# A sparse-attention and gated-convolution kernel: the first V on the software queue, mask rows by SBUF transfers, closing blocks in halves

## The chip, the core and the metric

The kernel runs on one core of a Trainium2 chip. The core has a matrix engine (TensorE, here PE; its weight loads, PEld, overlap its matmuls), VectorE (DVE), ScalarE (ACT), GpSimd (POOL) and SyncE (SP). Each engine runs its own instructions in the order in which the program put them down, and waits for other engines and for transfers by semaphores. Transfers (DMAs) are issued from SP and ACT, which have one hardware queue each, and from POOL, whose software queue also converts types on the way. All of them run on the same 16 DMA engines.

The metric is device time in microseconds. The kernel before takes 208.67 us, the median of three runs (208.65 to 208.9).

## What is computed

Block-sparse attention for 4 batch elements of 8 heads, 768 tokens and 64 channels, and behind it a gated convolution layer. Cut to what matters:

```python
scores = scale * np.matmul(q, k.transpose(0, 1, 3, 2))
mask = np.abs(blk_i - blk_j) <= window                    # blocks of 32 tokens
mask = mask | (blk_i == 0) | (blk_j == 0) | (blk_i == n_blocks - 1) | (blk_j == n_blocks - 1)
for qb in range(n_blocks):
    for kb in sampled_blocks[qb]:
        mask[qb * block:(qb + 1) * block, kb * block:(kb + 1) * block] = True
scores = np.where(mask, scores, -1000000000.0)
attn = softmax(scores)
x = np.matmul(attn, v)                                    # then heads side by side: 768 x 512 a batch element
h = np.maximum(x @ w_in, 0.0)                             # 512 -> 1024
conv_out = sum(conv_w[k] * shifted(h, k) for k in range(3))
out = h * sigmoid(conv_out) @ w_out                       # 1024 -> 512
```

`sampled_blocks` gives three more key blocks for each of the 24 query blocks. All heads share one mask.

## The kernel before

**Scores and mask.** Heads are taken in pairs, 16 pairs P = 0 to 15, four to a batch element. For each pair there is a slot, a tile t of 88 rows: rows 0 to 63 hold q and k transposed (24 chunks of 128 tokens: 12 of q, 12 of k), rows 64 to 87 hold 24 mask rows. With them one matmul (line 761) gives the scores and adds a large negative number where a query block may not see a key block: the q side carries the table of forbidden block pairs, the k side says which block a key is of. The mask rows are the same for every pair. There are five slots; pairs 0 to 4 are the first to use them.

**Units.** A unit is eight score blocks of 128 x 128: two score steps on PE into one of two PSUM tiles st, one exponential on ACT (line 773) into one of six tiles pt, and two steps of products with V on PE (line 798) into av. There are 144 units. They are ordered in segments: half of the queries (g = 0 or 1) of one batch element at a time. In the first segment a pair takes 4.5 units: unit 2 is the first that needs head 1 of pair 0, the second half of unit 4 is the first of pair 1, unit 9 the first of pair 2, the second half of unit 13 the first of pair 3.

**The layer behind.** Normalised rows (line 709) are transposed to xT; 18 units after its attention a segment goes through f1 (line 895), relu, the convolution on DVE (lines 953, 961) or, for the last segment, on PE (line 972), tanh on ACT, the gate gT (line 1008), and f2 (line 830) by `out_block`: for each block of 128 tokens eight matmuls of 512 columns, an eviction (ev) to a tile o2s and a store of 256 KB. Only the very last block is made in two halves of 256 columns.

**The order.** The steps are entered in a graph by `op` and `dma`, and numbered in that sequence. The string ORDER lists all 1,787 steps by two-character numbers; where a step may run on several engines a letter names one, and for a step that allocates a buffer a character gives its index. `put_down` follows that string. So the order on every engine, SP and POOL with their transfers among them, is written out by hand, and the costs and due times given in the source only served to find it.

**The start.** Pair 0 is loaded in 32 bits by the hardware queues: k in two halves (SP and ACT), q in two halves (ACT and SP), with the table of sampled blocks (`ld_sb`, SP, into sbi) ahead of the second half of q, then both heads of V (`ld_v0`, SP, into a tile of m) and the convolution weights (`ld_cw`). Casts on ACT and DVE (`cast_q`, `cast_k`) and PE transposes follow; `k_cp` and `q_cp` copy the transposes from PSUM into the slot. POOL makes iota and ident and then issues the loads of pairs 1, 2 and so on through the software queue. DVE builds the table of pairs: a1, a3 (from iota), a4 (first use of sbi), a5 in two halves into mtok (line 299). `nblk` (from ident) gives the k side. Mask rows are written into slot 0 by copies: `m_k` (k side, head 0), `m_q0` (q side, g = 0), `m_q1` (g = 1), `m_h1` (head 1: one copy of the q side, one of the k side), `m_r1` (g = 1 of head 1). Then `m_slot` copies all 24 rows from slot 0 to each of slots 1 to 4 on DVE. `m_back` stores a reordered copy for later pairs by two transfers from SP. `v_cp` brings V of pair 0 from 32 bits into its tile vt, on ACT between exponentials 1 and 2.

## Time and profile before

| | us |
|---|---|
| median of the runs | 208.67 |
| lowest and highest run | 208.65, 208.9 |
| span of the profiled execution, first to last instruction | 206.8 |

The page has no time of the profiled execution other than its span; 1.9 us of the median lie outside it. The granted TensorE clock is 0.997 of full speed over the span. The costliest groups of instructions, with busy time, mean duration of one in ns, and idle time of the engine ahead of them with what ended it:

```profile
L773 ACT ACTIVATE pt<-st 128x1024 bf16<-128x1024 f32 x144 | 140.6, 1048 | 2.4 <-PE st L761 1.3
L761 PE MATMUL st<-t 88*128 88x256 bf16 (+2 forms) x600 | 90.0, 267 | 1.6 <-ACT t L327 0.8
...
L798 PE MATMUL av<-vt,pt 128*128 128x65 bf16 x1152 | 58.4, 193 | 0.0
L895 PE MATMUL mix<-xT,winb 128*128 128x384 bf16 (+2 forms) x288 | 54.3, 308 | 0.3 <-ACT hE L915 0.2
```

Matmuls overlap, so the busy times of PE's groups add up to more than PE's busy time. `t<-mix` means that tile t is written from tile mix, buffer numbers left out.

### The profile page before, as it was taken

The page shows a single profiled execution, that of the slowest core. Times are in us where ns is not written, and L with a number is a line of the kernel's source. Part 1 is how long each engine was busy: PE and PEld are TensorE (multiplying, and loading weights), DVE is VectorE, ACT ScalarE, POOL GpSimd, SP SyncE. Part 2 cuts the span into 40 slices and gives each one's busy share as a digit, 9 for nine tenths or more (in the row PEclk, how much of TensorE's full clock was granted, in tenths as well). Part 3 has the DMA queues.
Part 4 walks back from the last instruction along what each step waited for, and adds up shares of the span by engine and source line. Part 5 has one row for each costly group of instructions (what it writes and reads, how often), then busy time and mean ns, then how long its engine had stood idle before and what let it go on. Part 6 is the DMA issues. An engine that isn't in the chain of part 4 may idle for free.

```text
span 206.8 us, 6250 instructions
## 1 busy us (share of the span) xinstructions
PE 199.3 (96%) x2418; PEld 142.7 (69%) x2418; DVE 186.4 (90%) x576; ACT 190.6 (92%) x252; POOL 61.9 (30%) x113
## 2 busy tenths in 40 slices
PE   7799999999999999999999999999999999999992
PEld 5587878887567766766676767676667667786750
DVE  7999989999999998999789989999999938999970
ACT  6999999999999999999989998999999979997751
POOL 8696735302843233316054153800000000000000
PEclk9999999999999999999999999999999999999998
DMA  6999999998699976999969659999235131010414
GB/s 156 196 196 185 181 165 132 187 113 77 78 127 142 179 102 93 147 139 193 194 96 107 138 77 170 151 144 130 67 115 87 22 120 51 3 51 5 152 53 153
DMA packets 49305, 25.20 MB, mean 122 GB/s; under 512 B 35100, under 2 KB 46332, under 8 KB 49276
## 3 DMA queue, kind: packets, MB, share of 16 engines
q0 software_dynamic: 19728, 11.05, 44.9%
q1 hardware_dynamic: 29260, 13.46, 33.9%
q8 instruction: 19, 0.31, 0.6%
q10 hardware_dynamic: 288, 0.30, 0.4%
q14 instruction: 10, 0.08, 0.1%
HBM read 23.09 MB, written 6.29 MB: 142 GB/s over the span
## 4 chain that ended last, share of the span: by engine, by line
PE 71%; DVE 14%; ACT 11%; issue 2%; ACTq 0%
PE st L761 22%; PE mix L830 18%; PE mix L895 16%; PE av L798 12%; ACT pt L773 8%; DVE t L331 3%; DVE m L953 3%; DVE m L961 2%; DVE gT L1008 1%; ACT t L327 1%; DVE xtok L709 1%; PE st L830 1%; DVE hE L917 1%; PE mix L728 1%; DVE m L1003 1%
## 5 line engine op out<-in xcount | busy, mean ns | idle before, releaser
L773 ACT ACTIVATE pt<-st 128x1024 bf16<-128x1024 f32 x144 | 140.6, 1048 | 2.4 <-PE st L761 1.3
L761 PE MATMUL st<-t 88*128 88x256 bf16 (+2 forms) x600 | 90.0, 267 | 1.6 <-ACT t L327 0.8
L761 PEld LDWEIGHTS <-t 88*128 88x128 bf16 x600 | 48.5, 97 | 21.4 <-issue 1.6
L798 PEld LDWEIGHTS <-pt 128*128 128x128 bf16 x1152 | 52.2, 97 | 11.5 <-ACT pt L773 1.0
L798 PE MATMUL av<-vt,pt 128*128 128x65 bf16 x1152 | 58.4, 193 | 0.0
L895 PE MATMUL mix<-xT,winb 128*128 128x384 bf16 (+2 forms) x288 | 54.3, 308 | 0.3 <-ACT hE L915 0.2
L953 DVE TENSOR_SCALAR m<-hE,cw 128x382 bf16<-128x382 bf16 (+2 forms) x192 | 48.8, 316 | 0.4
L830 PE MATMUL mix<-woutb,gT 128*128 128x512 bf16 x184 | 48.7, 379 | 0.2 <-DVE gT L1008 0.2
L961 DVE TENSOR_TENSOR m<-m 128x764 bf16<-128x764 bf16 (+2 forms) x64 | 33.8, 534 | 0.6
L895 PEld LDWEIGHTS <-winb 128*128 128x128 bf16 x288 | 24.4, 97 | 9.4 <-issue 0.8
L1000 ACT ACTIVATE m<-m 128x764 bf16<-128x764 bf16 (+2 forms) x32 | 26.8, 840 | 1.1 <-DVE m L961 1.0
L407 POOL COPY pace<-pt 1x1 bf16<-1x1 bf16 x24 | 9.6, 402 | 53.3 <-ACT pt L773 53.3
L830 PEld LDWEIGHTS <-gT 128*128 128x128 bf16 x200 | 17.3, 97 | 11.7 <-DVE gT L1008 1.1
L915 ACT ACTIVATE hE<-mix 128x384 bf16<-128x384 f32 (+2 forms) x36 | 17.7, 507 | 1.7 <-PE mix L895 1.6
L917 DVE TENSOR_SCALAR hE<-mix 128x384 bf16<-128x384 f32 x28 | 15.5, 557 | 4.1 <-PE mix L895 3.7
L1008 DVE TENSOR_TENSOR gT<-m,hE 128x764 bf16<-128x764 bf16 (+3 forms) x36 | 18.2, 511 | 0.6
L709 DVE TENSOR_TENSOR xtok<-av,rcp 128x384 bf16<-128x384 f32 (+2 forms) x36 | 18.1, 508 | 0.5
L239 POOL DMA_DIRECT2D nat<-in_q_dram x23 | 17.0, 738 | 2.1 <-issue 1.4
L331 DVE COPY t<-mix 64x384 bf16<-64x384 bf16 (+1 forms) x33 | 13.4, 413 | 0.7 <-PE mix L522 0.2
L327 ACT COPY o2s<-mix 128x512 f32<-128x512 f32 x17 | 9.9, 598 | 2.9 <-PE mix L830 2.7
L1003 DVE TENSOR_SCALAR m<-m 128x764 bf16<-128x764 bf16 (+3 forms) x36 | 12.1, 335 | 0.5 <-ACT m L1000 0.4
L239 POOL DMA_DIRECT2D vn<-in_v_dram x15 | 11.3, 756 | 1.9 <-DVE vt L331 1.4
(75 smaller groups left out, 118.4 us busy)
## 6 DMA issues: line engine op xcount, KB each, us to landing
out_dram<-o2s SPq DMA_DIRECT2D x23, 256.0 KB, 2.9
nat<-in_k_dram POOLq DMA_DIRECT2D x15, 192.0 KB, 4.2
vn<-in_v_dram POOLq DMA_DIRECT2D x15, 192.0 KB, 5.7
nat<-in_q_dram POOLq DMA_DIRECT2D x6, 192.0 KB, 4.9
winb<-in_moe_w_in_dram POOLq DMA_DIRECT2D x2, 512.0 KB, 7.3
woutb<-in_moe_w_out_dram POOLq DMA_DIRECT2D x4, 256.0 KB, 6.7
nat<-in_q_dram POOLq DMA_DIRECT2D x9, 96.0 KB, 5.2
nq<-in_q_dram POOLq DMA_DIRECT2D x6, 96.0 KB, 5.1
```

Of the source, the lines that this page charges most:

```text
L239: return op(name, {eng: occ}, lambda e: on(e).dma_start(out=dst(), in_=src), prio, deps, dma=(kind, service), **kw)
L331: nc.vector.tensor_copy(out=dst, in_=src)
L709: nm = op("norm", {"DVE": t_dps(128 * C)}, lambda e: nc.vector.tensor_tensor(out=xtok_t[xk.index][:, 0:C].rearrange("p c h d -> p h c d"), ...
L761: nc.tensor.matmul(out=st[:, 128 * x:128 * (x + n_)], lhsT=t[0:88, 12 + 6 * hh + kc, :], rhs=t[0:88, idx:idx + (n_ - 1) * (2 if P < NPE el ...
L773: nc.scalar.activation(out=pt_t[ptb.index][:, c0:c1], in_=st_t[stb.index][:, c0:c1], func=AF.Exp, bias=0.0, scale=0.125)
L798: nc.tensor.matmul(out=o[:, off:off + 65], lhsT=pt_t[ptb.index][:, 128 * x:128 * x + 128], rhs=V_t[vslot_b[P].index][:, hh, kc, 0:65], sta ...
L830: nc.tensor.matmul(out=acc(), lhsT=gT_t[gb.index][:, ffc, 128 * t:128 * t + 128], rhs=woutb[:, ffc, c0:c1], start=(ffc == 0), stop=(ffc == ...
L895: nc.tensor.matmul(out=mix_t[hb.index][:, w1 * y:w1 * y + w1], lhsT=winb[:, fc, 128 * ffc:128 * ffc + 128], rhs=xT_t[xt_buf[n].index][:, f ...
L953: nc.vector.tensor_scalar(out=m_t[cb.index][:, x, y, 0:w], in0=hE_t[heb.index][:, f0 + y, t0 + x:t0 + x + w], scalar1=cw[:, x, f0 + y:f0 + ...
L961: nc.vector.tensor_tensor(out=m[:, a_, :, 0:w], in0=m[:, a_, :, 0:w], in1=m[:, b_, :, 0:w], op=ALU.add)
L1000: th = [op("tanh", {"ACT": t_act(2 * w) + 0.04}, lambda e, cb=cb, w=w: nc.scalar.activation(out=m_t[cb.index][:, 0, :, 0:w], in_=m_t[cb.in ...
L1008: nc.vector.tensor_tensor(out=gT_t[gtb.index][:, f0:f0 + 2, t0:t1], in0=m_t[cb.index][:, 0, :, 0:w], in1=hE_t[heb.index][:, f0:f0 + 2, 1 + ...
```

## The change

- `ld_sb` moves from SP to POOL, ahead of iota; the second half of q follows k at once on SP.
- `ld_v0`, its 32-bit tile and its cast are gone. V of pair 0 is loaded by the software queue like that of the other pairs, behind q of pair 1, and `v_cp` copies it from 16 bits on either engine.
- The k side of head 1 (`m_hk`), the g = 1 rows of head 1 (`m_r1`) and the mask rows of slots 1 to 4 (`m_sk`, two `m_sq` and two `m_sr` for slot 1, `m_sp` for slots 2, 3 and 4) are written by transfers within SBUF, issued from SP, in place of copies on DVE.
- The scores of g = 1 wait for their own rows only.
- For the last batch element the blocks t = 3 and t = 4 are made in halves of 256 columns, as t = 5 is.
- ORDER is written anew as a whole, with 1,803 steps.

In the new string SP has, from the start: k, q, `m_hk`, `ld_cw`, `m_sq`, `m_sq`, `m_sk`, `m_r1`, `m_back`, `m_sp` (slot 2), `m_sr`, `m_sr`, `m_sp` (slot 4), `m_sp` (slot 3), then the transposing transfers. POOL has `ld_sb`, iota, ident, k and q of pair 1, V of pair 1, V of pair 0, k of pair 2 and on. ACT has `m_k`, three casts, `q_cp`, `m_q0`, two `k_cp`, and exponentials from there on. DVE has a1, nblk, a3, a4, `m_k`, the first a5, `k_cp`, `m_q0`, `k_cp`, `m_h1`, `cast_q`, the second a5, `q_cp`, `m_q1`, four copies for pair 1, ident24, `v_cp` of pair 0. PE has the scores of units 0 to 5 ahead of the first product with V. On PE the last steps are f2 of t = 3 and t = 4, second halves.

```diff
 ORDER = """
-0J0K1c1f00021010P0Q1Q01R0R0S0T0310V0/A0U14V1b0I0L0M0N0V0W0X1xA11zA1AA0405060708090a0b0c0d0e0f0g0h0i0j0k0l0m0n0o
...
+000L0O010P0J0K1U01g1f1V02103042401S10I0M05060708090a0b0c0d0e0f0Q0S1j0R1e1h2611O0272012i22k20+A1AA31CA1DA0g0h0i0j0k
...
-    vf = m_t[0].rearrange("p x y s -> p (x y s)")[:, 0:1536].bitcast(FP32)
...
-    ld_sb = op("ld_sb", {"SP": 0.46}, lambda e: nc.sync.dma_start(
-        out=sbi[64:MR], in_=sampled_blocks.bitcast(I32).rearrange("b r -> (b r)").unsqueeze(0).broadcast_to([NB, 6 * NB])),
-        -21, after=[k0], lat=1.8)
-    q1 = first_q(1, "SP", -20, [ld_sb])
+    ld_sb = dma("ld_sb", "POOL", lambda: sbi[64:MR], sampled_blocks.bitcast(I32).rearrange("b r -> (b r)").unsqueeze(
+        0).broadcast_to([NB, 6 * NB]), -21, kind="sw")
+    q1 = first_q(1, "SP", -20, [k0])
     ld_q0, ld_k0 = [q0, q1], [k0, k1]
-    ld_v0 = dma("ld_v0", "SP", lambda: vf.rearrange("p (h c) -> p h c", h=2),
-                v[0, 0:2].rearrange("h (p c) d -> p h (c d)", p=128), -18, service=1.6, after=[q1])
...
+    def rows_dma(name, prio, deps, dst, src):
+        return dma(name, "SP", dst, src, prio, deps, service=0.25)
+
+    def two_heads(x):
+        return x.unsqueeze(1).broadcast_to([NB, 2] + list(x.shape)[1:])
+
     m_h1 = [op("m_h1", {"DVE": 0.25, "ACT": 0.37}, lambda e: dcopy(e, T_t[0][64:88, 6:11:2], T_t[0][64:88, 0:5:2]), T(0), m_q),
-            op("m_h1", {"DVE": 0.45, "ACT": 0.69}, lambda e: dcopy(e, T_t[0][64:88, 18:24], T_t[0][64:88, 12:18]), T(0), m_k)]
-    m_r.append(op("m_r1", {"DVE": 0.25, "ACT": 0.37}, lambda e: dcopy(
-        e, T_t[0][64:88, 7:12:2], T_t[0][64:88, 1:6:2]), -5, m_r[0:1]))
+            rows_dma("m_hk", T(-2), m_k, lambda: T_t[0][64:88, 18:24].rearrange("j c s -> j (c s)"),
+                     T_t[0][64:88, 12:18].rearrange("j c s -> j (c s)"))]
+    m_r.append(rows_dma("m_r1", T(2), m_r[0:1], lambda: T_t[0][64:88, 7:12:2], T_t[0][64:88, 1:6:2]))
     mask_ready[(0, 1)] = m_h1
+    mask_g1 = {0: m_r}
     for s in range(1, NSLOT):
-        mr = [op("m_slot", {"DVE": 0.95}, lambda e, s=s: dcopy(e, T_t[s][64:88], T_t[0][64:88]),
-                 T(4.5 * s - 2.5), m_h1 + m_r, earliest=7.0 + 2 * s)]
+        mask_g1[s] = []
+        if s == 1:
+            mr = [rows_dma("m_sk", T(-1), m_k, lambda: T_t[1][64:88, 12:24].rearrange("j (h c) s -> j h (c s)", h=2),
+                           two_heads(T_t[0][64:88, 12:18].rearrange("j c s -> j (c s)")))]
+            for h in range(2):
+                mr.append(rows_dma("m_sq", T(0), m_q, lambda h=h: T_t[1][64:88, 6 * h:6 * h + 5:2], T_t[0][64:88, 0:5:2]))
+                mask_g1[s].append(rows_dma("m_sr", T(4), m_r[0:1], lambda h=h: T_t[1][64:88, 6 * h + 1:6 * h + 6:2],
+                                           T_t[0][64:88, 1:6:2]))
+        else:
+            mr = [rows_dma("m_sp", T(4.5 * s - 2.5), m_h1 + m_r, lambda s=s: T_t[s][64:88].rearrange("j c s -> j (c s)"),
+                           T_t[0][64:88].rearrange("j c s -> j (c s)"))]
         mask_ready[(s, 0)] = mask_ready[(s, 1)] = mr
...
                 qk_ready[(P, hh, g)] = (two + qk_ready[(P, hh, "k")] + mask_ready[(min(s, NSLOT - 1), hh)] +
-                                        (m_r if P == 0 else []))
+                                        (mask_g1[min(s, NSLOT - 1)] if g else []))
...
-        if P == 0:
-            def cp(e):
-                dcopy(e, V_t[vs.index][:, :, :, 0:64], vf.rearrange("p (h c d) -> p h c d", h=2, c=6))
-            v_ready[P] = op("v_cp", {"DVE": 0.5, "ACT": t_act(768)}, cp, due + 1, [ld_v0] + v_one, alloc=[vs], earliest=8.5)
-            in_turn("vs", v_ready[P])
-            return
...
-        in_turn("first" if P < NF else "v", lv)
+        if P == 0:
+            first_v.append(lv)
+        else:
+            in_turn("first" if P < NF else "v", lv)
...
     first_nq[0].after.append(first_q_sw[0])
+    first_v[0].after.append(first_q_sw[0])
...
-        halves = ((0, 256), (256, 512)) if last else ((0, 512),)
+        halves = ((0, 256), (256, 512)) if last or (b == B - 1 and t > 2) else ((0, 512),)
...
-                due + 3, [evo], uses=[ob], dma=("hw", 0.65 if not last else 0.4)))
+                due + 3, [evo], uses=[ob], dma=("hw", 0.65 if len(halves) == 1 else 0.4)))
```

More of the change, by code (lines that the diff above doesn't have):

```diff
@@ new lines @@
+2xV32gV5W15X2hV6k1676b21122V6t26w16x6c6y36g6h5Y06B06C6l6D41n1i23V6n26o5ZV6m16G16H6u6v6z6A6P06Q6E6F6I56U16V6J6K6p1
+6R06W11z53351546Z06+6S06T6/21q1s6L06M6N06qV6OV721736X6Yil174377078im7g17hio07947i5ip1o2LV41pinV00iqViJ07l07m7n070
+ir17q17r7175767s17v07w7a7x2iKiLiM7c1iN7d7b1iu0is7jiv7E1itA1iwV2ZV07k7F2t17J07o7K2uV2vViO7G3iP2A07p7tiD1iE2BV4iR1iT
+2CV7L47O17PiFA27Q57u7T07y7U7z7V02O12D07H07Y17Z7I7M7N7+13725538iS7A22EV2FViU2PV02QV7BiV7R850867Six08a18b8728c37Wiy7X
+7e17fV17/810izV3iQ0iW8018f08g8k18l2R1iA088iB89822SV2TV8d8h4310392323013a13k33b8m5iCV8t08u8e8i831iXiZ284V8y18z8v08j
@@ L62 @@
+hG1pDhz1hK1hAhjVpUpEAhR0hB0hCVp+hHhShLh+1qo1qphM0h/hT2qqAgi03qu0hUi30qvhVq13hN2q2p/q4q3hOqF0q5qHqGq0qwAhi4hP1hQA2q6
+q7hW0q8qV1hXqIqWic1idi11i2q90qaqbql1i55ie0qcqmi6qdA2i70qnAii81i9ifigqr0ia1qsibAqJih2qx2iiqzqyqtAjqKqf1qghY0qhhZVij0
+qiikArs0rtqAqLqBqN3qMqOqXqjA1rj1rkruAqCrlArp0rK1rLrqrM0rrAqDqPqErm1rnrv0roArwqkqepapgrx2r10rA1rBrF0rGqQqYrNryrOrzr2
+s50r71r/1r8rC0rH2qRqSrDqZrErIrJqTq+q/qUs6s0s1s7s8s2r9r0rar3r4s3V1s9ArbV2r5A3rP1rQrRrSrTA0rd0res4sar6rUrcrfrV1rgrhA
+rirWrXrYrZAr+
 """
@@ L402 @@
     k_first, slot_first, fine = {}, {}, {}
-    first_nq, first_q_sw = [], []
+    first_nq, first_q_sw, first_v = [], [], []
     def pace(u, prio):
```

73 lines of the change are left out of this document (31 added, 42 removed).

## The prediction

> **What bounds the kernel now.** I read the page first, then busy time by stage, then the chain of waits, then the first 14 us instruction by instruction. Page and stages:
>
> ```profile
> span 206.8 us, 6250 instructions
> ...
> PE 199.3 (96%) x2418; PEld 142.7 (69%) x2418; DVE 186.4 (90%) x576; ACT 190.6 (92%) x252; POOL 61.9 (30%) x113
> ```
>
> ```profile
> 0.00:7.60 7.60, 5.66 (x48) 4.42 (x49) 6.10 (x29) 5.20 (x10) 6.42 (x14) 1.00 0.77 169
> 7.60:23.00 15.40, 14.64 (x218) 11.56 (x217) 14.72 (x38) 15.34 (x17) 11.42 (x20) 1.00 1.33 190
> ...
> 30.00:190.00 160.00, 159.40 (x1954) 113.44 (x1952) 148.84 (x443) 155.15 (x201) 41.14 (x73) 1.00 0.79 112
> ...
> 203.00:207.00 4.00, 0.00 (x0) 0.00 (x0) 0.00 (x0) 0.54 (x1) 0.00 (x0) 0.84 0.30 110
> ```
>
> After stretch and length, the columns are busy time of PE, PEld, DVE, ACT and POOL, then the granted clock, the DMA engines' share and GB/s. From 30 to 190 us PE is busy 159.40 of 160, and the change leaves its work as it is: little is to be won there. From 7.6 to 23 ACT is busy 15.34 of 15.40, so that stage goes at the pace of the exponentials. Before 7.6 nothing is exponentiated, and after 203 only one eviction and the last store remain. A gain has to come from the first 23 us or the last four.
>
> The start, from the timeline (start, duration):
>
> ```profile
> 0.84 0.14 POOL L264 IOTA apart_i<- 88x24 int32 x1 [0.39 <-POOLq L1041]
> ...
> 1.21 0.42 SPq L255 DMA_DIRECT2D sbi<-in_sampled_blocks_dram  x1
> ...
> 1.26 0.29 POOL L266 TENSOR_SCALAR_AFFINE_SELECT ident<-ident 128x128 bf16<-128x128 bf16 x1 [0.28 <-DVE ident L224]
> ...
> 1.50 0.83 POOL L239 DMA_DIRECT2D nat<-in_k_dram  x1
> ...
> 2.07 0.43 SPq L239 DMA_DIRECT2D m<-in_v_dram  x1
> ...
> 2.37 0.55 DVE L286 COPY nblk<-ident 24x768 bf16<-24x768 bf16 x1
> ...
> 2.95 0.48 DVE L331 COPY t<-nblk 24x384 bf16<-24x384 bf16 x1
> ...
> 4.34 0.53 DVE L299 SCALAR_TENSOR_TENSOR A<-sbi,keyid,A 24x24 f32<-24x24 int32 x2
> ...
> 4.90 1.14 DVE L299 SCALAR_TENSOR_TENSOR mtok<-sbi,keyid,A 24x384 bf16<-24x384 int32 x2
> ...
> 5.54 0.60 ACT L327 COPY t<-mtok 24x128 bf16<-24x128 bf16 x2 [0.63 <-DVE mtok L299]
> ...
> 6.07 0.35 DVE L331 COPY t<-mix 64x384 bf16<-64x384 bf16 x1
> 6.17 0.47 ACT L327 COPY t<-mix 64x384 bf16<-64x384 bf16 x1
> ...
> 6.66 0.51 ACT L327 COPY t<-mtok 24x384 bf16<-24x384 bf16 x1
> 6.69 0.60 PE L761 MATMUL st<-t 88*128 88x384 bf16 x4 [0.78 <-ACT t L327]
> ...
> 7.08 0.50 ACT L327 COPY t<-t 24x384 bf16<-24x384 bf16 x1
> ...
> 7.61 1.94 ACT L773 ACTIVATE pt<-st 128x1024 bf16<-128x1024 f32 x2
> ...
> 9.16 0.34 PEld L460 LDWEIGHTS <-nat 128*128 128x128 bf16 x6 [0.27 <-DMA nat<-in_k_dram]
> ...
> 9.57 0.83 ACT L327 CAST vt<-m 128x768 bf16<-128x768 f32 x1
> ```
>
> The reader should see one relay: table of sampled blocks, A, mtok, mask rows, first scores at 6.69, first exponential (exponential 0) at 7.61. Then ACT stops for 0.83 us to cast the first V. Meanwhile the second pair's k, issued at 1.50, has released its transposes only at 9.16. From the chain of waits, exponentials 2, 5 and 9 (numbered from 0), and the last eviction:
>
> ```profile
> 10.40 0.93 ACT pt L773
> 11.38 0.64 PE st L761 x4
> ...
> 13.18 0.82 ACT pt L773
> ...
> 16.82 0.84 ACT pt L773
> ...
> 202.95 0.59 ACT o2s L327
> ```
>
> Exponential 4 follows the scores of 11.38, and heads this group of the timeline:
>
> ```profile
> 12.13 18.83 ACT L773 ACTIVATE pt<-st 128x1024 bf16<-128x1024 f32 x20
> ```
>
> The spacing in a steady run is (16.82 - 13.18) / 4 = 0.91 us.
>
> **Part 1, the sampled blocks first on GpSimd.** The order string, read out by numbering the steps in the order the program makes them, puts this DMA ahead of iota and ident on POOL. It takes iota's place at 0.84 and costs one issue, 0.83: iota moves to 1.67-1.81, ident to about 2.1, the second pair's k from 1.50 to 2.1. DVE's a1, nblk and a3 follow, and DVE is ready for the table at about 3.6. The old DMA had its table by 4.34 - 1.21 = 3.1 us after issue at the latest (DVE had no idle time before that step). The nearest software transfers, the 32 KB ones in the queue rows below, took 3.6. So the table is there at 3.9 to 4.4 against 4.34 at the latest now.
>
> **Part 2, the first scores.** DVE then does A (0.53), one m_k copy moved in here (0.48) and half of mtok (0.57): done at 5.5 to 6.0. Its k copy (0.35) and the shorter m_q copy, moved here from ACT (at most half of 0.60), end at 6.15 to 6.65, and the scores (0.60) at 6.8 to 7.3. ACT drops m_q1 and m_h1 (0.51 + 0.50) and takes two k copies (2 x 0.47) behind its m_q copy, ending at 6.8 to 7.25. Exponential 0 comes at 6.9 to 7.35; I take 7.2, a **gain of 0.4**. Unhindered at 0.91 each, exponential 2 would come at 9.0 instead of 10.40 and exponential 5 at 11.75 instead of 13.18. The two things that held them back, the V cast on ACT and k behind V, are gone.
>
> **Part 3, the first V.** Its cast becomes a copy from 16-bit on DVE, behind the second pair's k and q copies, at about 11. The new PE order multiplies by V only after the scores of unit 5, at about 11.5, and exponential 6 needs the buffer that this frees only at about 12.7. On POOL it stands behind the table, iota, ident and the second pair's k, q and V. With three issues of at most 0.83 after 2.1 its own starts by 4.6, and its kind took 5.7 (row below): 10.3. Hidden by six free exponential buffers; without that cover each tenth it is later than 12 is a tenth lost.
>
> **Part 4, mask rows by SBUF transfers.** DVE loses four 0.95 us copies and two small ones: 3.8 us off an engine that is not the limit here, worth nothing by itself. In their place the second pair's first scores (unit 4, second half) wait for three transfers on SP, and the third pair's (unit 9) for a chain of two. Rows:
>
> ```profile
> L331 DVE COPY t<-t 24x3072 bf16<-24x3072 bf16 x4 | 3.8, 952 | 0.1
> ...
> L343 SPq DMA_DIRECT2D mback<-t x2: 792/876/961, 6.2 to 7.2; - x2
> ...
> L239 SPq DMA_DIRECT2D t<-mback x5: 779/822/834, 35.1 to 93.1; - x5
> ...
> DMA to landing us min/median/max: 2.4/3.2/4.3
> ...
> nat<-in_q_dram POOLq DMA_DIRECT2D x4, 32.0 KB, 3.6
> ...
> vn<-in_v_dram POOLq DMA_DIRECT2D x15, 192.0 KB, 5.7
> ...
> 16.09 0.60 PE L761 MATMUL st<-t 88*128 88x384 bf16 x4
> ```
>
> These are rows of several views. The fourth is that of the o2s tiles: first loads and stores, all on the hardware queues. No landing of an SBUF-to-SBUF transfer is shown, so I bound it by this row, 2.4 to 4.3, and take the middle, 3.2, because this stretch is the busiest of the DMA engines. SP's new order is m_hk, conv weights, m_sq, m_sq, m_sk, m_r1, m_back (two issues), m_sp for the third pair, two m_sr, m_sp, m_sp. One waiting issue holds all behind it. m_hk waits for the m_k copy (5.0 to 5.4) and is landed at about 8.4, where unit 2 wants it at 8.3: nothing. The m_sq wait for the m_q copies, about 6.4. With 0.88 per issue of many short rows m_sk leaves at 8.2 and lands at 11.4 (10.6 to 12.5). Unit 4's second half then takes some 0.35 and exponential 4 comes at 11.8 (now 12.13), exponential 5 at 12.75 (now 13.18). So 0.4 of the possible 1.4 remains: **-0.4**, with ends of -1.3 and +0.7.
>
> m_r1 leaves at 9.0 (behind m_sk's 0.82; its rows are ready before) and lands at 12.2 (11.4 to 13.3). m_sp waits for that, leaves at 12.2 and lands at 15.4 (13.8 to 17.6). Now these scores run at 16.09; 0.4 earlier they want it at 15.7. **Nothing**, by a margin of 0.3; at the slow end 17.6 - 16.09 = 1.5 late against now.
>
> The Trainium skill (DMA: Bandwidth & Descriptors, section Anatomy of one DMA) has about 2.0 us fixed per transfer plus bytes over 436 GB/s. By that m_sk would land at about 10.4 and the sum come near the first rival's; the 3.2 above is what this trace's hardware queues show, with their data included.
>
> **Part 5, halved closing blocks.** The fourth and fifth token blocks of the last batch element are written in two halves of 256 columns. PE's columns stay the same. The last eviction shrinks by 0.59 - 0.37, and the last store has half the bytes:
>
> ```profile
> L327 ACT COPY o2s<-st x1: 372/372/372, 199.5 to 199.5; 128x256 f32<-128x256 f32 x1
> ...
> DMA to landing us min/median/max: 2.4/2.9/3.7
> ```
>
> This second row is that of the output stores. For the half store I take 2.6 for 2.9 (2.4 to 2.9). Two more issues of 0.42 on SP fall before the last eviction. **-0.5** (-0.2 to -0.7).
>
> **Part 6, the rest of the order.** Behind the start, fifteen evictions, relus and copies go from ACT to DVE and eight the other way. With PE busy 159.40 of 160 this wins at most 0.6 and could lose as much: **0**.
>
> **Sum.** 206.8 - 0.4 - 0.5 = 205.9 of span. The page gives no time for the profiled execution beside its span. The median of the runs, 208.67, lies 1.87 above it, which I keep: **207.8**.
>
> **Rivals.**
>
> *The transfers land fast.* At 2.4 us nothing holds unit 4, and the start keeps 1.3: 206.8 - 1.3 - 0.5 + 1.87 = **206.9**. For it: 2.4 is seen, and the rows are small. Against: the DMA engines are oversubscribed in that stretch (share 1.33 in the stage row, over 1).
>
> *The mask chain becomes the bound (slower).* At 4.3 each, m_r1 then m_sp land at 17.6; ACT and PE stand still at unit 9, +1.5, of which the end gives back 0.5: 206.8 + 1.5 - 0.5 + 1.87 = **209.7**. It decides from a landing later than 16.6, the 16.09 of now plus the gain at the end: 7.6 for the two, 3.8 each. For it: two landings in series ahead of a stage without slack. Against: 4.3 is the slowest of its row and a 96 KB load, while these are small.
>
> *The start's gain is given back.* If the new middle order costs PE the 0.4 gained at the start, and the halved store brings only the shorter eviction, 0.2: 208.67 - 0.2 = **208.5**, no change. For it: every engine's order is new and PE is full for 160 us, so that any misplaced wait costs. Against: ACT has more room than before.
>
> **Chances.** Forecast 0.42, fast landings 0.23, mask chain 0.20, gain given back 0.15. Within 0.2% (0.42 us, about what a measurement of this kernel can tell from no change) lies the last, with a small part of the forecast: same 0.19, faster 0.60, slower 0.21. The likeliest's own range is 207.2 to 208.5 (its ends of parts 2 and 5, and 0.3 either way in the middle). For 8 in 10 it must reach the fast case with most of its spread and the near part of the slow one: 206.6 to 209.5.
>
> **What would show it.** Exponential 0 near 7.2, and the V copy on DVE and not between exponentials on ACT: parts 2 and 3. A PE or ACT gap before exponential 4, ended by a DMA into the score operand tile t: part 4 as forecast; no gap there and exponential 5 near 11.75: fast landings. A gap at unit 9's scores ended by such a DMA: the mask chain. The last eviction 0.37 long and the span's end at most 3.0 after its store's issue: part 5. I am wrong if the table lands after 5, if V arrives after 12, or if the middle loses more than 0.6 of PE's busy time.

## The result: 3.3% slower, and the profile after

| | before | after |
|---|---|---|
| median of the runs, us | 208.69 | 215.61 |
| lowest and highest run | 208.65, 208.9 | 215.38, 216.51 |
| span of the profiled execution | 206.8 | 213.6 |
| granted clock over the span | 0.997 | 0.976 |

The ratio is 1.0338, with a 95% interval of 1.0318 to 1.0358. 207.8 was forecast, with a range up to 209.5. (Each kernel ran four times; ahead of the prediction stand three runs of the kernel before, hence 208.69 for 208.67.)

The page of the kernel after, its span and busy times:

```profile
span 213.6 us, 6292 instructions
...
PE 203.1 (95%) x2434; PEld 146.6 (69%) x2434; DVE 184.8 (87%) x579; ACT 189.2 (89%) x245; POOL 60.5 (28%) x115
```

PE's share has hardly moved, so the averages don't show what happened. The start of each exponential does. This table, read from the traces of the profiled executions, serves for the experiments too. A cell is the start minus that of the same exponential in the kernel before, and the last column is the difference of the spans. What e1 to k2 are is told under The experiments.

```
exponential      0      2      4      6      9     13     23    143    span
before (us)   7.61  10.31  12.13  14.10  16.82  20.62  29.94 187.16   206.8
after        +0.31  +2.00  +3.80  +4.82  +6.60  +7.18  +7.13  +7.98   +6.8
e1           +0.67  -0.05  +1.09  +2.20  +3.12  +3.84  +4.28  +5.36   +4.4
e2           +0.01  +0.50  +1.63  +1.70  +3.29  +3.60  +3.61  +3.81   +3.7
e3           +0.26  +2.22  +3.79  +3.62  +3.92  +7.44  +9.00 +11.03   +9.9
e4           +0.60  -0.28  -0.04  +6.04  +8.16  +8.00  +7.97  +9.68   +8.5
e5           +0.60  -0.27  -0.11  -0.26  +6.96  +6.81  +6.77  +7.53   +6.4
f1           -0.01  +0.12  +0.21  +0.28  +0.28  +0.28  +0.29  +0.41   +0.5
g1            0.00  +0.05  +0.06  +0.02  +0.01  +0.10  +0.10  +0.10   -0.4
f3           +1.65  +3.11  +3.11  +3.07  +3.07  +2.94  +2.97  +2.97   +3.0
g2           -0.01  +0.23  +0.23  +0.53  +0.58  +0.55  +0.55  +0.83   +0.9
h1           +0.67  -0.04  +1.10  +1.44  +2.41  +3.24  +3.67  +4.80   +3.8
h2           -0.20  -0.91  +0.23  +0.53  +1.56  +2.38  +2.81  +3.53   +2.5
k1           +0.40  -0.39  +0.61  +1.80  +2.65  +2.50  +2.47  +2.99   +1.8
k2           +0.30  +0.80  +3.21  +4.23  +5.00  +6.22  +6.18  +7.91   +6.7
```

All of the loss of the kernel after is there by exponential 13: 7.18 us. From 23 to 143 another 0.85 is lost, and behind the last exponential 1.2 is won. The first stage in the timeline of the kernel after (start, duration, engine, instruction, idle time ahead of it and what ended it):

```profile
1.29 0.69 POOL L238 DMA_DIRECT2D sbi<-in_sampled_blocks_dram  x1 [0.84 <-POOLq L1050]
...
4.79 0.53 DVE L294 SCALAR_TENSOR_TENSOR A<-sbi,keyid,A 24x24 f32<-24x24 int32 x2 [0.28 <-DMA sbi<-in_sampled_blocks_dram]
...
5.93 0.92 SPq L238 DMA_DIRECT2D t<-t  x1
...
7.56 3.42 SPq L238 DMA_DIRECT2D t<-t  x4
...
11.77 0.50 PE L770 MATMUL st<-t 88*128 88x256 bf16 x3 [2.25 <-DMA t<-t]
...
13.39 0.34 DVE L326 COPY vt<-vn 128x768 bf16<-128x768 bf16 x1
...
15.31 0.58 PE L770 MATMUL st<-t 88*128 88x384 bf16 x2 [1.34 <-DMA t<-t]
...
16.30 4.22 SPq L238 DMA_DIRECT2D t<-t  x5
...
19.71 1.04 PE L770 MATMUL st<-t 88*128 88x128 bf16 x4
...
23.64 0.60 PE L770 MATMUL st<-t 88*128 88x128 bf16 x4
...
27.31 0.39 PE L770 MATMUL st<-t 88*128 88x384 bf16 x2 [0.55 <-DMA t<-t]
```

`t<-t` on SPq are the row transfers, `[... <-DMA t<-t]` on PE the waits for them. `m_hk` is issued at 5.93, and PE may begin unit 2 at 11.77: 5.8 us. The rows of slot 1 hold unit 4 until 15.31, those of slot 3 hold unit 13 until 27.31. The same four scores take 1.04 at 19.71 and 0.60 at 23.64. The chain of waits names the other two row transfers:

```profile
10.20 6.08 DMA t<-t
...
19.78 7.49 DMA t<-t
```

`m_r1` took 6.08, and the rows of slot 3 took 7.49. Slot 3 is the last of five row transfers that SP issues together, and they land one behind the other, from 21.7 to 27.3. The stage in stretches of 2 us (columns as in the prediction):

```profile
9.00:11.00 2.00, 0.51 (x9) 0.28 (x6) 1.89 (x5) 1.02 (x1) 1.35 (x2) 1.00 1.26 183
11.00:13.00 2.00, 1.23 (x10) 0.98 (x11) 0.49 (x3) 0.69 (x1) 0.00 (x0) 0.81 1.42 188
13.00:15.00 2.00, 0.97 (x5) 0.26 (x2) 0.70 (x3) 1.35 (x2) 0.97 (x2) 0.50 1.24 199
...
17.00:19.00 2.00, 2.00 (x25) 1.71 (x24) 0.98 (x5) 1.10 (x2) 1.65 (x3) 0.50 1.25 165
19.00:21.00 2.00, 2.00 (x24) 1.66 (x22) 1.11 (x2) 1.10 (x2) 0.75 (x2) 0.50 1.15 182
21.00:23.00 2.00, 2.00 (x25) 1.64 (x24) 1.05 (x4) 1.41 (x2) 1.80 (x5) 0.63 1.01 134
23.00:30.00 7.00, 6.43 (x115) 5.45 (x113) 6.04 (x20) 6.40 (x8) 2.24 (x6) 1.00 1.04 150
```

In the holds PE is busy 0.51, 1.23 and 0.97 of 2, and the granted clock falls to 0.50. It stays there for about 10 us, at least four of them with PE busy without a gap: exponentials 6, 7 and 8 now wait 0.78, 0.90 and 0.59 for scores. The DMA share is over 1 throughout, the condition under which the row transfers have to land.

The middle and the end of the kernel after, from its timeline:

```profile
151.58 0.84 ACT L1009 ACTIVATE m<-m 128x764 bf16<-128x764 bf16 x1 [1.18 <-DVE m L970]
...
152.14 0.48 PE L904 MATMUL mix<-xT,winb 128*128 128x384 bf16 x2 [0.93 <-DVE hE L926]
...
210.42 0.37 ACT L322 COPY o2s<-mix 128x256 f32<-128x256 f32 x1 [0.28 <-PE mix L839]
```

At 152 us PE and ACT wait about 1 us for a relu and a sum on DVE. The last eviction is 0.37 long and ends at 210.79, 2.8 before the end of the span, where before 0.59 and 3.2 stood.

### The profile page after: what moved, and what is told of

It is laid out like the page before. It is cut to its first block, busy times and chain, and to the rows that moved or that the text cites. A ratio compares the mean times of both kernels' runs of the same rounds, so it can differ in the third digit from the quotient of the medians.

```text
span 213.6 us, 6292 instructions
## 1 busy us (share of the span) xinstructions
PE 203.1 (95%) x2434; PEld 146.6 (69%) x2434; DVE 184.8 (87%) x579; ACT 189.2 (89%) x245; POOL 60.5 (28%) x115
## 4 chain that ended last, share of the span: by engine, by line
PE 47%; DVE 19%; DMA 14%; ACT 10%; issue 6%; SPq 2%; POOL 1%; POOLq 0%; DVEq 0%; ACTq 0%
PE st L770 13%; PE mix L839 13%; PE mix L904 11%; ACT pt L782 7%; PE av L807 7%; DMA t<-t 6%; DVE m L962 5%; DVE m L970 3%; DMA vn<-in_v_dram 3%; DMA stg<-nat 3%; DVE t L326 3%; SPq L238 2%; DVE hE L926 2%; DMA sbi<-in_sampled_blocks_dram 2%; DVE gT L1017 1%
## 5 line engine op out<-in xcount | busy, mean ns | idle before, releaser
L770 PE MATMUL st<-t 88*128 88x256 bf16 (+2 forms) x600 | 92.7, 273 | 4.4 <-DMA t<-t 4.1
L807 PEld LDWEIGHTS <-pt 128*128 128x128 bf16 x1152 | 58.0, 98 | 16.6 <-ACT pt L782 1.3
L807 PE MATMUL av<-vt,pt 128*128 128x65 bf16 x1152 | 65.4, 195 | 0.1
L904 PE MATMUL mix<-xT,winb 128*128 128x384 bf16 (+2 forms) x288 | 56.1, 307 | 1.1 <-DVE hE L926 0.9
L962 DVE TENSOR_SCALAR m<-hE,cw 128x382 bf16<-128x382 bf16 (+2 forms) x192 | 49.9, 313 | 0.1
L839 PE MATMUL mix<-woutb,gT 128*128 128x512 bf16 (+1 forms) x200 | 49.1, 362 | 0.3 <-DMA nat<-in_q_dram 0.2
L904 PEld LDWEIGHTS <-winb 128*128 128x128 bf16 x288 | 23.3, 97 | 8.6 <-issue 1.5
L839 PEld LDWEIGHTS <-gT 128*128 128x128 bf16 x216 | 18.0, 97 | 9.9 <-DVE gT L1017 1.5
L418 POOL COPY pace<-pt 1x1 bf16<-1x1 bf16 x24 | 8.4, 350 | 55.2 <-ACT pt L782 55.1
L924 ACT ACTIVATE hE<-mix 128x384 bf16<-128x384 f32 (+2 forms) x35 | 17.2, 503 | 0.6 <-PE mix L904 0.3
L238 POOL DMA_DIRECT2D vn<-in_v_dram x16 | 11.7, 732 | 4.9 <-DVE vt L326 3.6
L326 DVE COPY t<-stg 64x1536 bf16<-64x1536 bf16 x19 | 11.0, 581 | 0.4
```

Source lines behind the costliest of these rows:

```text
L238: return op(name, {eng: occ}, lambda e: on(e).dma_start(out=dst(), in_=src), prio, deps, dma=(kind, service), **kw)
L326: nc.vector.tensor_copy(out=dst, in_=src)
L770: nc.tensor.matmul(out=st[:, 128 * x:128 * (x + n_)], lhsT=t[0:88, 12 + 6 * hh + kc, :], rhs=t[0:88, idx:idx + (n_ - 1) * (2 if P < NPE el ...
L807: nc.tensor.matmul(out=o[:, off:off + 65], lhsT=pt_t[ptb.index][:, 128 * x:128 * x + 128], rhs=V_t[vslot_b[P].index][:, hh, kc, 0:65], sta ...
L839: nc.tensor.matmul(out=acc(), lhsT=gT_t[gb.index][:, ffc, 128 * t:128 * t + 128], rhs=woutb[:, ffc, c0:c1], start=(ffc == 0), stop=(ffc == ...
L904: nc.tensor.matmul(out=mix_t[hb.index][:, w1 * y:w1 * y + w1], lhsT=winb[:, fc, 128 * ffc:128 * ffc + 128], rhs=xT_t[xt_buf[n].index][:, f ...
```

## The experiments

Theory M: a row transfer needs not the 2.4 to 4.3 us of the prediction but about 6, because bulk loads of the software queue use the same DMA engines; the time that PE is held, and the half clock behind it, are the loss. Rivals: V comes too late through the software queue (V), the new order costs by itself (O), the table on GpSimd costs (T).

### e1 and e2: the rows alone, undone and done

e1 is the kernel after with all row transfers turned back into copies on DVE, g = 1 rows still separate:

```diff
-        return dma(name, "SP", dst, src, prio, deps, service=0.25)
+        return op(name, {"DVE": 0.4}, lambda e: dcopy(e, dst(), src()), prio, deps)
```

> The changed kernel with part 4 alone undone: every mask row is spread by a DVE copy again (m_hk and the m_k copy ahead of a4, the rows of pair 1 behind q_cp of pair 0, the rows of slots 2 to 4 between later copies), V, the table, the halves and the rest of the order as changed. Theory M (the mask transfers land late, hold PE at units 2 and 4, and the pause halves the clock): 207.8 to 209.2, no wait of PE on a DMA into t, granted clock 0.99 or more. Rival V (the first V on the software queue costs the time): 213 or more. Rival O (the new order of the rest costs it): 212 or more, with exponential 9 near 17.5 and the loss spread behind it.

e2 is the kernel before with the row transfers of the kernel after in place of its copies, issued from SP behind `ld_v0`, and nothing else:

```diff
-        mr = [op("m_slot", {"DVE": 0.95}, lambda e, s=s: dcopy(e, T_t[s][64:88], T_t[0][64:88]),
...
+            mr = [rows_dma("m_sp", T(4.5 * s - 2.5), m_h1 + m_r, lambda s=s: T_t[s][64:88].rearrange("j c s -> j (c s)"),
+                           T_t[0][64:88].rearrange("j c s -> j (c s)"))]
```

> The kernel before with part 4 alone: mask rows by SBUF transfers from SP in the sequence of the changed kernel, everything else as before (V on SyncE's queue ahead of them). Theory M: 213 to 218, PE waits of 1.5 us or more on a DMA into t at units 2 and 4, clock down to about half behind them. Rivals V and O: within 1 us of the kernel before, 207.7 to 209.7.

e1 took 212.87 us (ratio 1.0218, 1.0165 to 1.0270): 2.7 of the 6.9 come back, not all. No theory has this: theory M had 209.2 at most, and of rival O the time is met (212 or more) but not the place, since exponential 9 starts at 19.94 and not near 17.5. e2 took 212.99 in two runs (1.0203, 1.0169 to 1.0238): the rows alone cost 4.3 in the old order, next to theory M's 213 and far from the rivals' 209.7. Timeline of e2:

```profile
3.67 0.89 SPq L238 DMA_DIRECT2D t<-t  x1
...
10.27 0.72 PE L770 MATMUL st<-t 88*128 88x256 bf16 x5 [0.73 <-DMA t<-t]
...
13.34 0.38 PE L770 MATMUL st<-t 88*128 88x384 bf16 x2 [1.08 <-DMA t<-t]
...
19.42 0.60 PE L770 MATMUL st<-t 88*128 88x384 bf16 x4 [1.58 <-DMA t<-t]
```

The rows of head 1 leave 2.3 us earlier than in the kernel after and still take 6.6. Three holds follow, at units 2, 4 and 9, each ended by a transfer. PE's granted clock was 1.00 over this execution, so its 3.7 us are waits alone; that theory M expected half clock here was wrong. In e1 the place of the wait at unit 4 is taken by another:

```profile
12.80 0.38 PE L769 MATMUL st<-t 88*128 88x384 bf16 x2 [1.09 <-DVE t L327]
```

```profile
11.00:13.00 2.00, 0.59 (x5) 0.29 (x3) 1.91 (x7) 1.20 (x2) 0.00 (x0) 1.00 1.42 200
...
15.00:17.00 2.00, 2.00 (x24) 1.70 (x22) 1.77 (x9) 1.23 (x2) 2.00 (x5) 0.50 0.59 81
```

DVE is busy 1.91 of 2 and hasn't room for the rows: the rows of slot 1 and `m_q1`, which was ACT's before, stand on it from 9.57 on, ahead of the k copies of pair 1, which start at 10.89 instead of 9.71. PE idles and loses its clock here too.

### e4 and e5: the software queue held

Both are the kernel after with one small copy on GpSimd that reads the k rows of slot 1 and so holds POOL until `m_sk` has landed. In e4 every load behind k and q of pair 1 stands behind it; in e5 V of pair 0 goes ahead of it.

```diff
+    op("hold", {"POOL": 0.12}, lambda e: nc.gpsimd.tensor_copy(out=held_t[64:88], in_=T_t[1][64:88, 12, 0:1]), 0)
```

> The changed kernel with POOL held behind k and q of pair 1 until the k rows of slot 1 (m_sk) are landed, so that the software queue is empty while m_hk, the m_sq and m_sk run. All later loads come later, V of pair 0 too. If the software queue's load is what makes the row transfers late: m_hk is landed within 3 us of its issue, PE does not wait for it at unit 2, m_sk is landed by 12.5, and V is late instead (first product with V at 14 or later). If the transfers are slow by themselves: PE waits at unit 2 as before, to about 11.7, and the whole is later than 216.

> The kernel after, with V of pair 0 right behind k and q of pair 1 on the software queue and all later software loads held until the k rows of slot 1 (m_sk) have landed. Theory M (a row transfer takes 6 us only when bulk loads of the software queue stand on the same DMA engines): rows land as in the run that held the queue earlier, exponentials 2 to 5 within 0.4 of the kernel before's, V copied by 12 and exponential 6 free; the loads of pairs 1 (V), 2 and 3 come late instead. At least 4 less than the kernel after, 208 to 211.6, if k of pair 2 lands by 17. Rival O (the new order costs by itself): exponentials 2 to 5 on time, but 212 or more, lost behind exponential 6.

e4 took 217.34 in its one run, e5 215.39 (1.0340, 1.0305 to 1.0374). Timeline and stretches of e5:

```profile
7.48 3.43 SPq L239 DMA_DIRECT2D t<-t  x4
...
8.21 6.67 ACT L783 ACTIVATE pt<-st 128x1024 bf16<-128x1024 f32 x7
...
11.58 0.34 DVE L327 COPY vt<-vn 128x768 bf16<-128x768 bf16 x1
11.66 0.31 POOL L1036 COPY held<-t 24x1 bf16<-24x1 bf16 x1 [7.06 <-DMA t<-t]
...
18.34 0.82 PE L472 MATMUL mix<-ident,nat 128*128 128x128 bf16 x6 [4.64 <-DMA nat<-in_k_dram]
```

```profile
7.00:9.00 2.00, 2.00 (x28) 1.58 (x26) 1.84 (x6) 1.94 (x4) 0.00 (x0) 1.00 0.48 85
9.00:11.00 2.00, 1.71 (x18) 1.14 (x16) 1.87 (x6) 2.00 (x4) 0.00 (x0) 1.00 0.21 46
...
19.00:21.00 2.00, 2.00 (x25) 1.66 (x24) 1.11 (x2) 0.45 (x1) 1.47 (x4) 0.50 1.18 212
```

This is the core of the matter. With the DMA share at 0.48 and 0.21 instead of 1.09 and 1.26, no row transfer holds anything: seven exponentials run without a gap, exponential 6 is 0.26 earlier than before, V is there at 11.58. `m_sk`, the last but one of the four issues from 7.48 on, starts at 9.24 and frees the copy on GpSimd at 11.66. The trace records the landing of every transfer by its semaphore; from the start of the issue to the last landing, in us:

| | `m_hk` | `m_sq` | `m_sq` | `m_sk` | `m_r1` | `m_sp` of slot 2 |
|---|---|---|---|---|---|---|
| kernel after | 5.8 | 5.8 | 5.4 | 5.9 | 6.1 | 5.4 |
| e4 | 2.2 | 2.1 | 2.0 | 2.3 | 2.0 | 4.6 |
| e5 | 2.6 | 2.1 | 2.0 | 2.3 | 2.0 | 5.4 |

The last column shows it within the same runs: in e4 and e5 these rows are issued at 12.7, when the loads run again (from 12.1). So the same transfers take 2.0 to 2.6 without the bulk loads and 4.6 to 6.1 with them. Then the bill comes: k of pair 2, held back, lands at 18.3, PE stands still for 4.6 us and loses its clock on top, and the run is no faster than the kernel after. In e4, where V was held too, exponential 6 waits until 20.14 instead; what was expected of its rows and of V came true. My expectation of 208 to 211.6 for e5 was missed, since it took k's landing by 17 for granted.

### e3 and h1: the clock

e3 is the kernel after with 45 and 30 matmuls on a constant tile put into the two holds, so that PE isn't idle there. h1 is e1 with 36 of them between 10.7 and 13.7.

```diff
+    more = [op("keep", {"PE": 0.056}, lambda e: nc.tensor.matmul(
+        out=av_t[1][:, 0:128], lhsT=warm[:, 0:128], rhs=warm[:, 0:128], start=True, stop=True), 0) for _ in range(75)]
```

> The changed kernel with 75 more filling matmuls of 128 columns on PE (45 ahead of the scores of unit 2, 30 between the two score steps of unit 4), as long as the two holds, so that PE is not idle while it waits. Nothing else differs. If the halved clock of 12 to 22 us is a cost of its own that the idle PE brings on: the clock stays at 1.00, exponential 9 comes near 20.5 to 21 instead of 23.42, and the time is 212 to 213.5. If the clock falls for another reason (the load, or a given place in time): the clock is down as before and the time is 215.5 to 217.

> The run with the rows copied on DVE (the kernel after without part 4), with 36 idle matmuls of 128 columns on PE in the stretch from 10.7 to 13.7 where PE stood still and after which its granted clock was 0.50 from 15 to 17. Theory C (the half clock is a cost of its own wherever no transfer sets the time behind it): clock 1.00 from 13 to 19, exponential 8 some 1.5 to 1.9 earlier than 19.03, and 211.0 to 211.6 instead of 212.87. Rival (something behind it gives the same time back, as the rows of the fourth pair did in the kernel after): exponential 8 earlier, the run 212.4 to 213.2.

e3 took 218.74 (1.0479, 1.0458 to 1.0500), 3 us more than the kernel after and more than either expectation. The first 45 matmuls came to stand ahead of unit 1's last scores, so exponential 1 is 2.5 later than in the kernel after, but exponential 4 is where it was. Its timeline:

```profile
15.00 9.51 ACT L784 ACTIVATE pt<-st 128x1024 bf16<-128x1024 f32 x10 [1.45 <-PE st L772]
...
27.58 0.39 PE L772 MATMUL st<-t 88*128 88x384 bf16 x2 [3.50 <-DMA t<-t]
```

The clock was kept: ten exponentials run at full pace, and exponential 9 is 2.7 us earlier than in the kernel after (+3.92 against +6.60). So the half clock did cost 2.7 there. But the rows of slot 3 land at 27.58, as in the kernel after (27.31). What the clock won is lost in a hold of 3.5, whose idle PE then loses the clock behind it (half from 28.6 to 32.1). In the kernel after, then, the half clock was cover for a row transfer that was later still. Behind exponential 23 e3 loses another 1.2 against the kernel after; that was not followed.

h1 took 212.25 (1.0166, 1.0149 to 1.0183). Exponential 8 came 1.55 earlier than in e1, as theory C has it, but the end only 0.6, between the theory and its rival; the rest went in the next waits (ACT's for scores at 19.23 is 0.73). The intervals of the two runs overlap, so the price of the clock in e1 is known only roughly.

### f3 and h2: the table on GpSimd

f3 is the kernel before with part 1 alone; h2 is e1 with part 1 undone; k2 is the kernel after with part 1 undone.

```diff
-    ld_sb = op("ld_sb", {"SP": 0.46}, lambda e: nc.sync.dma_start(
...
+    ld_sb = dma("ld_sb", "POOL", lambda: sbi[64:MR], sampled_blocks.bitcast(I32).rearrange("b r -> (b r)").unsqueeze(
+        0).broadcast_to([NB, 6 * NB]), -21, kind="sw")
```

> The kernel before with part 1 alone: the table of sampled blocks first on GpSimd, the second half of q at once behind k on SP. In the kernel after a4 started at 4.79 against 4.34. Theory T (the software transfer lands later than the hardware one did): first exponential 0.3 to 0.5 later, 208.9 to 209.4. Rival (the prediction's part 1, the table not later, q earlier): 208.2 to 208.7.

> The run with the rows copied on DVE, and with the table of sampled blocks back on SP's hardware queue, iota first on GpSimd again. In the kernel before, the table on GpSimd alone cost 2.7. Theory T (it costs here too: exponential 0 back from 8.27 to 7.4-7.7, everything behind it 0.5 to 1.0 earlier): 211.8 to 212.4 instead of 212.87. Theory T2 (the earlier chain also takes away the idle PE and the half clock behind it): 209.5 to 211. Rival (the new order of DVE and ACT has absorbed the late table; q behind the table on SP is as late): 212.6 to 213.2.

> The kernel after with one thing undone: the table of sampled blocks on SP's hardware queue as before, iota first on GpSimd. Theory H (the row landings set the time up to the fourth pair, so an earlier start is lost in their waits): exponential 0 at 7.4 to 7.7, exponential 13 within 0.6 of 27.8, 214.8 to 215.8. Rival A (the prices add; every row transfer leaves as much earlier as its source is ready): 213 to 214.3, exponential 13 at 26.2 to 27.

f3 took 211.44 (1.0126, 1.0101 to 1.0151), far more than either theory. Timeline of f3:

```profile
3.66 0.59 DVE L284 COPY nblk<-ident 24x768 bf16<-24x768 bf16 x1
...
4.28 0.70 ACT L325 COPY t<-nblk 24x384 bf16<-24x384 bf16 x1 [1.33 <-DVE nblk L284]
5.01 1.18 ACT L325 CAST nat<-o2s 128x192 bf16<-128x192 f32 x3
...
8.21 1.01 PE L759 MATMUL st<-t 88*128 88x384 bf16 x4 [0.35 <-ACT t L325]
```

It isn't the table itself. Behind its issue, iota and ident are 1.2 later, so `nblk` starts at 3.66 instead of 2.37, and on ACT the k-side mask copy that needs it stands ahead of the casts of q and k; exponential 0 follows at 9.26, 1.65 late. By exponential 2 it is 3.11, and there the clock comes in: the first four score matmuls take 1.01 instead of the 0.60 of the kernel before, as at half clock in the kernel after (1.04), and the trace's record of full clock begins at 13.22, in the other runs between 4.1 and 7.1. So the 2.7 are the path and a late clock together; the runs lie at 210.9 to 211.0 and at 211.9 to 212.4. In the kernel after the new order of DVE and ACT has most of that back (exponential 0 at +0.31). h2 took 211.00 (1.0137, 1.0082 to 1.0192), 1.9 less than e1: a larger gain than theory T has, and just the edge of T2's range. In its profile exponential 2 is 0.91 earlier than before, a gain such as parts 2 and 3 were to bring. Its start doesn't repeat exactly: k1 below has the same one and exponential 0 at +0.40, where h2 has -0.20. In h2 full clock is granted from 4.31 on, in k1 from 6.98, and until then three of PE's transposes take 0.53 instead of 0.33. So the 1.9 is uncertain by some 0.6. k2 took 215.58 (1.0326, 1.0273 to 1.0379): nothing won, as theory H has it. But exponential 9 was 1.6 and exponential 13 still 0.96 earlier than in the kernel after, more than H allows; exponential 13 at 26.84 is what rival A had. At exponential 143 the two are level, and where the gain was lost was not followed. Its four runs go from 213.93 to 216.78, so what the table's place costs in the kernel after is known to about 1 us only, and in the median it is nothing.

### f2 and g2: the first V

> The kernel before with part 3 alone: the first V by the software queue behind k and q of the second pair, copied from 16 bits on DVE, first products with V behind the scores of unit 5; rows, table and closing blocks as before. Theory V (the late first V costs): V lands after 11, exponentials 6 or 7 wait for it and it is 209.5 to 211. Rival R (the V part wins and rows and clock alone make the loss): exponential 2 comes 0.5 to 1.4 earlier than 10.31 since ACT has no cast and k of the second pair is not behind V, and the run is 207.3 to 208.5. Rival O: with the exponentials at their pace the order of the middle takes any gain back, 208.5 to 208.9.

f2 put V of pair 0 into the tile of pair 3's V, whose load stood ahead of the copy in the order. So the copy waited for that load and took pair 3's V for pair 0, at 16.01, and exponential 6 came 5.19 late: 215.84 (1.0334). It is a run on a late V, no answer to the question. g2 puts the load of pair 3 behind the copy:

```diff
-    ld_v0 = dma("ld_v0", "SP", lambda: vf.rearrange("p (h c) -> p h c", h=2),
...
+        if P == 0:
+            first_v.append(lv)
```

> The kernel before with the V part alone, V of pair 0 with a vn buffer of its own until its copy is done (the load of pair 3's V goes behind that copy). Theory Q (exponential 2 hangs on DVE's q copy behind the first m_slot, not only on the V cast): exponentials 0 to 5 as in the kernel before, within 0.3. If V is copied by 12.7, nothing is held and the run is 208.3 to 209.0. Rival V (the software queue brings V after 13): exponential 6 waits, 209.5 to 211. Rival R (ACT free of the cast): 207.3 to 208.3.

g2 took 209.65 (1.0043, 1.0030 to 1.0055): 0.9 slower, more than theory Q's 209.0. Its timeline:

```profile
8.45 1.13 DVE L327 COPY t<-t 24x3072 bf16<-24x3072 bf16 x1
9.61 0.35 DVE L327 COPY t<-av 64x384 bf16<-64x384 bf16 x1
...
10.54 3.77 ACT L767 ACTIVATE pt<-st 128x1024 bf16<-128x1024 f32 x4 [1.00 <-PE st L755]
...
11.78 0.36 DVE L327 COPY vt<-vn 128x768 bf16<-128x768 bf16 x1
12.96 1.13 PE L792 MATMUL av<-vt,pt 128*128 128x65 bf16 x32
```

V is in place at 11.78 and holds nothing, so theory V falls. But the gain isn't there either (theory Q): without the cast, ACT waits 1.00 for unit 2's scores, whose q copy stands on DVE behind the first `m_slot`. Two things ended at the same time before, and taking one away showed the other. The products with V, put off to one block of 32, then delay unit 6 (exponential 6 at +0.53); the other 0.3 was not followed.

### f1 and g1: the closing blocks

```diff
-        halves = ((0, 256), (256, 512)) if last else ((0, 512),)
+        halves = ((0, 256), (256, 512)) if last or (b == B - 1 and t > 2) else ((0, 512),)
```

> The kernel before with part 5 alone: t = 3 and t = 4 of the last batch element in halves, nothing else moved. Theory of the prediction: the last eviction 0.37 instead of 0.59 and a store of half the bytes, 0.2 to 0.7 us less, so 208.0 to 208.5 (ratio 0.9967 to 0.999), the last exponential where it was at 187.2. The kernel after shows 0.22 for the eviction and 0.42 for the store, which would be 208.1. Rival: the second halves' extra weight loads and the extra store ahead of the last one on SP's queue take it back, 208.5 to 208.9.

g1 has `t == 4` in place of `t > 2`.

> The kernel before with only its last written block (t = 4 of the last batch element) in halves; t = 3 stays whole, so no matmul of another block moves behind the last gate. Theory (part 5's gain of 0.64 is real and t = 3's second half, moved behind the last gate for want of a third mix buffer, took 0.43 to 0.7 of it in the run with both): 207.9 to 208.3, ratio 0.996 to 0.998. Rival (halves bring nothing, the extra weight loads or the store queue take it): 208.6 to 208.9.

f1: 208.82, ratio 1.0001 (0.9991 to 1.0011). g1: **208.25, ratio 0.9977 (0.9968 to 0.9986)**, the one kernel of the study that beats both. PE's last group in the kernel before, then in f1:

```profile
199.27 3.65 PE L830 MATMUL mix<-woutb,gT 128*128 128x512 bf16 x16
```

```profile
199.66 4.39 PE L830 MATMUL mix<-woutb,gT 128*128 128x256 bf16 x32
```

Two mix buffers are there. With t = 3 in halves, its second half can take a buffer only when others are done, so half of its eight matmuls run behind the last gate, where before the first half of t = 3 ran ahead of it: 1,024 columns more, 0.46 by the 3.65 / 16 of one 512-column matmul. (A row shows the shape of its first matmul; by shape, f1's 32 are 28 of 256 columns and 4 of 512.) The group as a whole is 0.74 longer, which eats the shorter eviction and store. With t = 4 alone in halves nothing moves.

### k1: late rows by transfer

k1 is h2 with the rows of slots 2, 3 and 4 by three transfers from SP, the early rows still copies on DVE.

```diff
-            mr = [rows_dma("m_sp", T(4.5 * s - 2.5), m_h1 + m_r, lambda s=s: T_t[s][64:88], lambda: T_t[0][64:88])]
+            mr = [dma("m_sp", "SP", lambda s=s: T_t[s][64:88].rearrange("j c s -> j (c s)"),
+                      T_t[0][64:88].rearrange("j c s -> j (c s)"), T(4.5 * s - 2.5), m_h1 + m_r, service=0.25)]
```

> The run with the rows on DVE and the table on SP, but the whole-slot rows of slots 2, 3 and 4 by three transfers from SP as in the kernel after; the early rows (head 1, slot 1) stay copies on DVE. These transfers leave at about 12 to 15. Theory D (DVE's copies for the later slots make the waits at exponentials 9 and 13): exponentials 0 to 5 as in that run (7.41 to 13.65), DVE 2.9 freer, and at 7 us a landing slot 2's rows come at 19 to 20 and hold unit 9 by 1 to 2: 210.5 to 212. Rival (no hold: transfers of some 3 us where the software queue has less ahead of them): 209 to 210.3. Rival M+ (each landing 7.5, slot 3 at 24 or later): 212 to 214.

k1 took 210.94 (1.0127, 1.0078 to 1.0176), as much as h2. Timeline:

```profile
12.68 2.43 SPq L239 DMA_DIRECT2D t<-t  x3
...
17.64 9.27 ACT L783 ACTIVATE pt<-st 128x1024 bf16<-128x1024 f32 x10 [0.72 <-PE st L771]
```

No wait on a row transfer is left: ten exponentials from 17.64 on run without a gap, where h2 lost 0.8 between exponentials 9 and 13. The trace fits theory D about DVE's copies, and there is no hold at unit 9 as it had. The three transfers took 3.1, 4.4 and 5.3 us, and the work that needs them was far enough away. But k1's profile began 0.6 later and had the clock at half from 13.8 to 17.2, which h2's had not, and was 1.1 behind it at exponential 9. The medians come out alike.

## Why the prediction was wrong

**Part 4, the size of the row landings.** This is the step that failed. "I bound it by this row, 2.4 to 4.3, and take the middle, 3.2." The row was that of loads and stores on the hardware queues, most of them in parts of the kernel where the DMA share is below 1. Measured: 5.8 for `m_hk`, 6.08 for `m_r1`, 7.49 for slot 3, and 6.6 in e2. The prediction had the cue, the share of 1.33, but used it only to take the middle of its row and against the fast rival, and not to move the upper bound. The rows nearest in circumstance, the software loads at 3.6 to 5.7 which it shows beside the other, would have given a hold of up to 2.6 us at unit 2 (5.2 + 5.7 against 8.3), and more behind it. e4 and e5 show the cause: with the bulk loads held, the same transfers take 2.0 to 2.6 and hold nothing.

The Trainium skill (DMA: Bandwidth & Descriptors, section Queues, rings and completion order) says that each DMA engine goes round between the queues that have work, a packet at a time. By that a small transfer on SP's queue would not have to wait for the whole backlog of GpSimd's. At this load the trace shows a long wait all the same: the first data of `m_hk` moved at 10.21, 4.3 us after its issue, and in e5 at 7.50, 1.6 after. How much of that is a turn of other packets and how much the backlog, no run here shows. The estimate that ends part 4 (Trainium skill, same page, section Anatomy of one DMA, where it is given for the software queue) puts `m_sk` at 2.2 us; that is right with the loads held, 2.3, and far off with them, 5.9.

**Part 4, `m_hk`.** "Is landed at about 8.4, where unit 2 wants it at 8.3: nothing." It came at 11.7: 2.00 late at exponential 2 instead of a gain.

**Part 4, the chain `m_r1` to `m_sp`.** The break-even of 3.8 each was passed: 6.08 and 7.49. The slower rival had the right mechanism and too small a price, 209.7, since it saw its first hold at unit 9 and took 4.3 as the worst. In the kernel after unit 9 was not held; the holds came at units 2, 4 and 13.

**The clock was left out.** No case asked what a PE that waits does to the clock. In the kernel after it was at half for about 10 us, worth 2.7 up to exponential 9 (e3). There it hid under slot 3's landing, so that it is not a term of its own in the total; h1 against e1 shows it as one, with the reserve made there. The Trainium skill (TensorE: Matmul & The Clock Gate, Part 1) halves the clock after an idle window of about 3.4 us and gives it back after a busy one, with windows that run freely. This case agrees in kind: 0.51 of 2 busy from 9 to 11 and half clock from 12.2; PE full from 17 on and the clock back at 22.5. The stretches at half clock last 3.4, 6.8 or 10.2 us in the runs here. But PE was not wholly idle before the clock fell.

**Parts 1 and 2.** The table was there at 4.7, not 3.9 to 4.4, and its issue began at 1.29 and not at 0.84. Exponential 0 came 0.31 later instead of 0.4 earlier. That the path over iota, ident and `nblk` would be longer was computed, but not followed to the casts on ACT; alone it cost 1.65 at exponential 0 and, with the late clock, 2.7 in all (f3). A small misreading: exponential 2 started at 10.31, and the 10.40 of the chain is where the chain enters it.

**Part 3.** Right that V is hidden: its load landed at 10.34 in the kernel after, as forecast (10.3), and the copy at 13.39 waited for DVE's earlier steps; in g2 the copy ran at 11.78. Wrong that without the V cast exponential 2 would come earlier: g2.

**Part 5.** The last eviction (0.37) and the landing behind it (2.8 instead of 3.2) came as forecast, 0.64 together. That PE's columns "stay the same" was right, but not that their place does: alone, the part brought nothing (f1).

**Part 6.** 0 was forecast, with 0.6 either way: 0.85 was lost between exponentials 23 and 143. The wait at 152 us is a relu that the new order has on DVE. It was not tried alone.

**The sum of the parts.** Alone, in the old order, they cost 4.3 (rows), 2.7 (table, part of it the late clock), 0.9 (V) and 0.1 (halves), 8.0 together against 6.9. Taken out of the kernel after one by one, rows then table, they give back 2.7 and 1.9, and 2.3 stay. DVE's lack of room for the rows is part of that rest (h2 and k1); how it divides among V, the order and the clock was not settled.

## What to carry to other kernels

A transfer that replaces a copy takes the latency of the DMA engines at that moment: here 2.0 to 2.6 us without bulk loads, and 4.6 to 7.5 with them and a DMA share over 1. Bound it by the slowest transfers of the same stretch, and use it only where the reader is further away than that. A wait on PE can have a second price, the granted clock behind it (2.7 us up to exponential 9 here), and both can hide under a later wait, so that undoing one shows nothing. Of two things that end together, removing one wins nothing: look for what is next before counting the gain.
